# Attention and a two-layer network on one core: zero products and a small sigmoid at the start, two loads from another queue, and a wider choice of PSUM banks

## The chip, the cores and the metric

The kernel runs on one core of a Trainium2 chip. The metric is the device time of one execution in microseconds. A core has TensorE for matrix products, VectorE, ScalarE and GpSimd for elementwise work, and SyncE, from whose queue this kernel issues its transfers; each engine runs its own instructions in order and waits on semaphores for the others. TensorE writes only to PSUM, which the kernel uses as eight banks of 512 float32 columns.

## The reference

Eight batches, 12 heads, 448 positions, 64 columns a head. Attention takes a sigmoid in the place of a softmax; its output, laid out as 448 rows of 768, goes through a mixing of low rank along the sequence and then a two-layer network, both added on.

```python
scores = q @ k.T / sqrt(64) - log(448)
x = sigmoid(scores) @ v                    # heads side by side: (8, 448, 768)
u = x + ((x.T @ U) @ V).T                  # U (448, 32), V (32, 448)
out = u + relu(u @ w_ch1) @ w_ch2          # (768, 3072), (3072, 768)
```

## The kernel before

The 12 heads of a batch are worked off as six **pairs**. A pair's scores fill four tiles, j = 3, 0, 1, 2: three tiles of 128 keys for both heads, two banks each, and one bank that holds the last 64 keys of both heads. ScalarE's sigmoid brings each tile to SBUF, and TensorE multiplies with v. Batch 0 and half of batch 1 do this in float32; the rest, and all of the network, splits each float32 into two float16 parts and takes three products. The weights come as 64-bit words: VectorE decodes them in twelve groups (six for each layer, `decode`, L874), scales and splits them, and parks them in DRAM for the later batches. Batches 0 to 3 run the network in plain form (`ffn_in`, `ffn_out`), 4 to 7 in a form with seven products instead of eight, behind everything else.

The order is not written by hand. Every operation is handed to a `Plan` with an engine, an estimated cost, what it reads and writes, and a due position (`pos`). `Plan.order` (L136) plays the operations through in a model of the engines while the program is built: it always takes the operation that can start first, and among those that can start at the same time the one with the lowest due position. What it finds is then the fixed order of instructions on each engine and queue. So a changed due time, cost or choice of buffer changes the order on any engine. The due times come from constants at the head of the file (L54 to L77): `START` and `AT` place the network's groups, `D1` the pairs of batch 1, `TWO_AT` the attention of batch 2, `SOONER`, `B0` to `B5` that of batches 3 to 7, `PREP` and `BOUNDS` the preparation of a pair, `DECODE` the weights, `MIX_1`, `MIX_2` and `MIXED1` the mixing, `U_STEP` and `STEP_I` forms of inputs and weights for the last batches.

What the change and the prediction touch:

- `load` (L390) issues a transfer from SyncE's queue. `loads` (in front of `pair`, L537) brings a pair's k and q, each by head (64 partitions), into one of three `qk` buffers, and v into one of two.
- Batch 0's six pairs are the first work of TensorE, with due positions from -100 on. Between them run the decoding of the first weights, the mixing of batch 0 (`mix`) and, from 82 us, the first chains of the network.
- `mixing` (L496) sets up the identity, the sigmoid's bias and U and V; it writes `vst`, the scaled V in float16 (448 columns), late, at 67 us.
- PSUM: the network's chains take banks 0 to 3 (`PF`, L349) during the first pass over the groups; scores take banks 4 to 7, or all eight where `early` (L683) is true, that is in batch 0 and in pairs 0 and 1 of batch 1. A tile is given back once its last reader is done.
- Matmuls are issued on L407 and transposes on L410; VectorE's and ScalarE's helpers make L417, L420 and L679 stand for many operations.

Of the kernel before, what the change touches and what calls it, by code (L numbers as in the profile page):

```python
# [37 lines left out]
P = 128  # L38
D = 64
S = 448  # L40
# [10 lines left out]
DOWN = 2.0 ** -24  # L51
DOWN_H = 2.0 ** -22
WHOLE = (6, 6, 6, 0, 0, 0, 0, 0)
D2, TWO_AT = 24.207, 77.057  # L54
PLAIN = 4
LATER = [3, 4, 5, 6, 7]
TOGETHER = (2, 3, 4, 5)
# [4 lines left out]
PIPE = {P * PIECE * 8: 2.5, D * S * 4: 0.53, D * D * 4: 0.13, D * P * 4: 0.1, P * 2 * WE * 2: 4.8, P * 42 * P * 2: 4.1, P * 24 * P * 2: 1.92, P * 6: 2.2, P * 1536: 1.3}  # L62
SWITCH, TURN, LAND, RATE = 0.09, -2.054, 2.2, 0.33e6
TINY = 235
B0, B1, B2, B3, B4, B5 = 2.934, -0.318, -0.301, -2.832, -1.273, 1.274
HOLD_PE, HOLD_DVE, HOLD_ACT, HOLD_POOL, HOLD_SP = 0.029, 0.0, 0.0, 0.0, 0.0
HOLD = lambda e: {"PE": HOLD_PE, "DVE": HOLD_DVE, "ACT": HOLD_ACT, "POOL": HOLD_POOL, "SP": HOLD_SP}[e]

ROOM0, ROOM, AHEAD, BEFORE, D1, SOONER = 89.279, 30.792, 47.233, 54.769, 4.497, 70.468
PREP, BOUNDS, VALUES, SECOND, MIXED = 19.043, 11.533, 1.917, 3.17, 7.744  # L70
LOW_POOL = ()
MIXED1, MIX_1 = 1.829, -0.567
MIX_2, EV_IN, EV_OUT, A_OFF = 11.002, 33.543, 3.656, 0.056
START, DECODE = 30.42, 56.642
U_AT, U_STEP = 3.172, 3.581
LEAD, SUMS, STEP_K, STEP_I, FFN_LEAD = 5.196, 28.387, 3.783, 5.28, 4.0
ORDER = "iiiioiooiioiooiioiooiooo"  # L77


# [19 lines left out]
class Plan:  # L99
# [13 lines left out]
    def op(self, eng, cost, fn, reads=(), writes=(), pos=0.0, slack=0.0, land=0.12, after=(), port=False, dma=0.0, shape=(0, 0)):  # L113
        deps = set(after)
        for k in reads:
            deps.update(self.wrote.get(k, ()))
        for k in writes:
            deps.update(self.wrote.get(k, ()))
            deps.update(self.read.get(k, ()))
        i = len(self.ops)  # L120
        for k in reads:
            self.read.setdefault(k, []).append(i)
        for k in writes:
            self.wrote[k], self.read[k] = [i], []
        tiles = []
        for k in (*reads, *writes):
            t = k[0] if isinstance(k, tuple) else k
            if isinstance(t, Tile) and t not in tiles:
                tiles.append(t)
                t.users.append(i)  # L130
                if t.at is None:
                    t.at = (pos, i)
        self.ops.append((eng, cost, fn, sorted(deps), pos, slack, land, tiles, port, dma, shape))
        return i
# [123 lines left out]
def fused_kernel(ctx: ExitStack, tc: tile.TileContext, q, k, v, wu, wv, w1, w2, out):  # L258
# [128 lines left out]
            small[name] = [Buffer(tiny(n)) for _ in range(ring_)]  # L387
        return plan.tile(name, small[name])

    def load(dst, src, n, reads, writes, pos, land=LAND):  # L390
        op("SP", 0.6 if n in (D * S * 4, D * D * 4, D * P * 4) else 0.36, lambda: nc.sync.dma_start(out=dst(), in_=src()), reads, writes, pos, land=land, dma=PIPE.get(n, n / RATE))  # L391

    def dve(cost, fn, reads, writes, pos):
        op("DVE", cost, fn, reads, writes, pos)
# [5 lines left out]
    def act(cost, fn, reads, writes, pos):  # L400
        op("ACT", cost, fn, reads, writes, pos)
# [4 lines left out]
    def matmul(*x, **y):  # L406
        plan.made.append(nc.tensor.matmul(*x, **y))  # L407
# [109 lines left out]

    def shifted(at):  # L520
        pool(0.5, lambda: nc.gpsimd.memset(ux, 0.0), (), ["ux", "vraw"], at)
        dve(0.25, lambda: nc.vector.tensor_copy(ux[0:64, 0], ua[0:64, 3]), [("ua", i) for i in range(4)] + ["ux"], ["ux"], at)
        load(lambda: ux[64:128, :, 3], lambda: ua[0:64, :, 0], 0.08e6, [("ua", 0), "ux"], ["ux"], at)
        load(lambda: ux[0:64, 1:4, 3], lambda: ua[64:128, 0:3, 0], 0.08e6, [("ua", 0), "ux"], ["ux"], at)
# [12 lines left out]
    def loads(b, p, early, stacked):  # L537
        qk, v32 = plan.tile("qk", QK), plan.tile("v", V32)

        for h in range(2):  # L540
            for i, src in ((1, k), (0, q)):
                load(lambda i=i, h=h: qk.x[rows_of(h), i * S : i * S + S], lambda src=src, h=h: src[b, p, rows_of(h), h, :],
                     D * S * 4, [], [(qk, i, h)], early)
            if stacked:
                load(lambda h=h: qk.x[rows_of(h), 2 * S :], lambda h=h: kin[b, p, rows_of(h), h, S - D :], D * D * 4, [], [(qk, 2, h)], early)
        if stacked:
            x = v[b, p]
            ends = bass.AP(x.tensor, x.offset + 384, [[512, D], [512 * D + D, 2], [1, D]])
            load(lambda: v32.x[:, :3], lambda: v[b, p, :, :3], P * 384 * 4, [], [(v32, 0)], early + 0.1)
            for i in range(2):  # L550
                load(lambda i=i: v32.x[rows_of(i), 3, :], lambda: ends, D * P * 4, [], [(v32, 1 + i)], early + 0.1)
        else:
            load(lambda: v32.x, lambda: v[b, p], P * 512 * 4, [], [(v32, 0), (v32, 1), (v32, 2)], early + 0.1)
        return qk, v32, [(qk, i, h) for i in range(2) for h in range(2)]
# [48 lines left out]
    def pair(b, p, at, d):  # L603
# [76 lines left out]
                out_(), in_(), AF.Sigmoid, bias=bias_s, scale=c if whole else c.x), kin + ["bias"] + kc, kout, pos)  # L680

        sc = {}
        early = b == 0 or b == 1 and p < 2  # L683
        for n, j in enumerate((3, 0, 1, 2)):
            here = at + (d * (n // 2) / SECOND if b else 0.0)
            if b == 0:
# [35 lines left out]
    def new_u(b):  # L722
        u32s[b] = [plan.tile(f"u{'abc'[min(b, 2)]}{c}", [(UA, UB, UC)[min(b, 2)][c]]) for c in range(NP)]
        mxs[b] = sm("mx", NP) if b < PLAIN else sm(f"mx{b}", NP, 1)
# [511 lines left out]
            out_(u[0, 1], 1, 0)  # L1236


    mixing()
    new_u(0)  # L1240
    for p in range(NP):
        pair(0, p, 6.0 * p - 100.0, 6.0)
# [148 lines left out]
```

## Time and profile before

| | us |
|---|---|
| median of the timed runs | 1564.28 (1563.14 to 1565.6, three runs) |
| profiled execution | 1560.01 |
| its span | 1558.2 |
| TensorE busy in the span | 1548.8 |
| VectorE / ScalarE / GpSimd busy | 1112.4 / 776.1 / 351.5 |
| moved by DMA | 303.82 MB, 195 GB/s on average |

A profile is of one execution. A line of the order of time has the start in us from the span's start, the length, the engine, the line of the kernel, the operation, what it writes and reads (`out<-in`), its shape, how many like ones are merged into the line, and in brackets the idle time of the engine before it with what ended it. Names such as `qk__101` are buffers: the first pair's k and q. PE is TensorE's matmul part, PEld its loading of weights, DVE VectorE, ACT ScalarE, POOL GpSimd, SPq the queue of SyncE. A line of the view by stretches gives, for each stretch, its length and then the busy time of PE, PEld, DVE, ACT and POOL with their number of instructions, the granted clock, the share of the DMA engines' time and GB/s. A line of the waits gives the waiting engine, what it waited for, us in total, times, and the longest.

### The profile page before, as it was taken

To read this page: it belongs to the slowest core of one execution; us is meant where nothing else is said; L and a number is where in the kernel's file an instruction comes from. 1 tells how busy PE (TensorE), PEld (TensorE's weight loads), DVE (VectorE), ACT (ScalarE), POOL (GpSimd) and SP (SyncE) were. 2 spreads that over 40 slices of the span, in tenths; PEclk is the share of its full clock that TensorE was granted. 3 is DMA by queue.
4 is the path that set the end of the run, shared out by engine and by line. 5 is a ranking of instruction groups with operands and counts; after the bars stand their busy time and mean duration, and the time that the engine had idled before them with its cause. 6 is when DMAs were issued, how large, how long until landed. Compare 5 with 4: busy or idle time off the path is not lost.

```text
span 1558.2 us, 23417 instructions
## 1 busy us (share of the span) xinstructions
PE 1548.8 (99%) x8651; PEld 759.9 (49%) x8651; DVE 1112.4 (71%) x1831; ACT 776.1 (50%) x1269; POOL 351.5 (23%) x429
## 2 busy tenths in 40 slices
PE   8999999999999999999999999999999999999999
PEld 3334444455444454444444544555555555555554
DVE  4688987566667777787887677777767777565656
ACT  6566466444567557777878356342323614131310
POOL 0100000003551652221221451055662500000000
PEclk9999999999999999999999999999999999999999
DMA  9599777435658995776777775967773673333321
GB/s 280 174 310 316 220 265 242 148 96 159 184 153 220 250 280 145 204 174 168 183 222 221 213 244 161 264 217 238 237 253 137 212 259 108 107 109 140 107 106 72
DMA packets 217554, 303.82 MB, mean 195 GB/s; under 512 B 138336, under 2 KB 188384, under 8 KB 206176
## 3 DMA queue, kind: packets, MB, share of 16 engines
q1 hardware_dynamic: 217440, 302.33, 62.9%
q8 instruction: 68, 1.11, 0.3%
q14 instruction: 46, 0.38, 0.1%
HBM read 232.10 MB, written 76.04 MB: 198 GB/s over the span
## 4 chain that ended last, share of the span: by engine, by line
PE 57%; ACT 0%; DMA 0%; issue 0%; DVE 0%; SPq 0%; ACTq 0%
PE banks L407 57%; DMA v__105<-v_in 0%; ACT at L679 0%; PE banks L410 0%; ACT w L839 0%; ACT a L705 0%; DVE ub__79 L420 0%; SPq L391 0%; ACT junk L473 0%; ACTq L473 0%; DVE tiny L832 0%; ACT uc__83 L711 0%; DVE tiny L442 0%
## 5 line engine op out<-in xcount | busy, mean ns | idle before, releaser
L407 PEld LDWEIGHTS <-w__92 128*128 128x128 f16 x1683 | 163.3, 98 | 157.4 <-issue 6.7
L407 PEld LDWEIGHTS <-w__91 128*128 128x128 f16 x1620 | 157.0, 98 | 152.5 <-issue 8.5
L407 PEld LDWEIGHTS <-w__94 128*128 128x128 f16 x1620 | 157.0, 98 | 151.0 <-issue 8.6
L407 PEld LDWEIGHTS <-w__93 128*128 128x128 f16 x1557 | 150.4, 98 | 147.9 <-issue 11.5
L679 ACT ACTIVATE at<-banks,tiny 128x896 f32<-128x896 f32 x120 | 127.0, 1098 | 42.0 <-DVE a L420 18.9
L420 DVE SCALAR_TENSOR_TENSOR a<-at,a 64x896 f16<-64x896 f32 (+1 forms) x120 | 135.5, 1145 | 13.0 <-ACT a L705 8.3
L407 PE MATMUL banks<-h__96,w__94 128*128 128x448 f16 x690 | 139.7, 353 | 0.0
L407 PE MATMUL banks<-h__95,w__93 128*128 128x448 f16 x678 | 136.9, 353 | 0.4 <-ACT h__96 L939 0.4
L417 POOL TENSOR_SCALAR tiny<-tiny 128x1 f32<-128x1 f32 (+1 forms) x90 | 30.0, 342 | 354.4 <-DVE tiny L417 328.3
L1014 POOL TENSOR_TENSOR w<-w 128x384 f32<-128x384 f32 x96 | 105.8, 1102 | 5.2
L407 PE MATMUL banks<-us__89,w__92 128*128 128x448 f16 x498 | 101.3, 353 | 0.0
L407 PE MATMUL banks<-us__89,w__91 128*128 128x448 f16 x501 | 101.2, 353 | 0.0
L407 PE MATMUL banks<-us__90,w__91 128*128 128x448 f16 x471 | 95.1, 353 | 0.0
L407 PE MATMUL banks<-us__90,w__92 128*128 128x448 f16 x471 | 94.6, 353 | 0.0
L705 ACT ACTIVATE a<-at 128x896 f16<-128x896 f32 x90 | 82.6, 950 | 0.2
L679 ACT ACTIVATE a<-banks,tiny 128x448 f32<-128x448 f32 (+1 forms) x72 | 63.0, 910 | 27.6 <-PE banks L407 27.5
L1010 POOL TENSOR_TENSOR w<-w 128x384 f32<-128x384 f16 x48 | 46.6, 1000 | 95.5 <-DVE xnt L1018 70.7
L938 ACT ACTIVATE r__98<-banks 128x448 f32<-128x448 f32 x48 | 26.0, 541 | 70.6 <-PE banks L407 68.1
L938 ACT ACTIVATE r__97<-banks 128x448 f32<-128x448 f32 x48 | 25.9, 539 | 60.9 <-PE banks L407 60.7
L407 PE MATMUL banks<-h__95,w__94 128*128 128x448 f16 x264 | 54.3, 353 | 0.0
L407 PE MATMUL banks<-h__96,w__93 128*128 128x448 f16 x249 | 51.3, 353 | 0.0
L407 PEld LDWEIGHTS <-stg__109 64*128 64x128 f16 (+1 forms) x690 | 32.6, 102 | 38.1 <-issue 17.0
(897 smaller groups left out, 2833.0 us busy)
## 6 DMA issues: line engine op xcount, KB each, us to landing
w<-w_in SPq DMA_DIRECT2D x48, 768.0 KB, 6.2
forms<-xnt SPq DMA_DIRECT2D x24, 768.0 KB, 4.4
w__92<-forms SPq DMA_DIRECT2D x13, 1344.0 KB, 5.7
w__91<-forms SPq DMA_DIRECT2D x12, 1344.0 KB, 5.9
w__94<-forms SPq DMA_DIRECT2D x12, 1344.0 KB, 5.8
w__93<-forms SPq DMA_DIRECT2D x11, 1344.0 KB, 5.9
forms<-scratch SPq DMA_DIRECT2D x144, 96.0 KB, 5.0
w__91<-scratch SPq DMA_DIRECT2D x7, 1536.0 KB, 8.1
```

Of the source, the lines that this page charges most:

```text
L407: plan.made.append(nc.tensor.matmul(*x, **y))
L417: return eng.tensor_scalar(out=out, in0=in_, scalar1=s1, scalar2=s2, op0=op0, **kw)
L420: return nc.vector.scalar_tensor_tensor(out=out, in0=in0, scalar=s, in1=in1, op0=op0, op1=op1)
L679: act(cost, lambda: nc.scalar.activation(out_(), in_(), AF.Sigmoid, bias=bias_s, scale=c if whole else c.x), kin + ["bias"] + kc, kout, pos)
L705: act(0.95, lambda a=a, to=to: nc.scalar.activation(half(a, 0), to.x, AF.Copy, scale=A_UP), kto, [(a, 0)], here + A_OFF)
L938: act(0.54, lambda: nc.scalar.activation(r.x, ph.x[:, :S], AF.Relu, scale=DOWN_H), [ph], [r], pos - EV_IN)
L1010: pool(1.0, lambda j=j: nc.gpsimd.tensor_tensor(out=t.x[:, j], in0=quarter(j, 0), in1=quarter(j, 1), op=ALU.add), [(w, j, 0), (w, j, 1)] i ...
L1014: pool(1.0, lambda o_=o_, x=x, y=y, sub=sub: nc.gpsimd.tensor_tensor(out=t.x[:, o_], in0=t.x[:, x], in1=t.x[:, y], op=ALU.subtract if sub ...
```

## The change

Four things change.

1. Ahead of everything, VectorE sets `vst` to zero, and TensorE multiplies it with itself nine times into one bank (`waking`). The result isn't read; `vst` is written anew later.
2. ScalarE does a sigmoid of one column into `junk`, once the bias is there (`table`).
3. The two loads of q for pair 0 of batch 0 are issued from ScalarE's queue.
4. Pairs 2 and 3 of batch 1 count as `early`, so their scores may take all of PSUM. Beside it some fifteen of the constants for due times have other values.

```diff
@@ -51,7 +51,7 @@
 DOWN = 2.0 ** -24
 DOWN_H = 2.0 ** -22
 WHOLE = (6, 6, 6, 0, 0, 0, 0, 0)
-D2, TWO_AT = 24.207, 77.057
+D2, TWO_AT = 24.207, 73.828
 PLAIN = 4
 LATER = [3, 4, 5, 6, 7]
 TOGETHER = (2, 3, 4, 5)
@@ -62,18 +62,18 @@
 PIPE = {P * PIECE * 8: 2.5, D * S * 4: 0.53, D * D * 4: 0.13, D * P * 4: 0.1, P * 2 * WE * 2: 4.8, P * 42 * P * 2: 4.1, P * 24 * P * 2: 1.92, P * 6: 2.2, P * 1536: 1.3}
 SWITCH, TURN, LAND, RATE = 0.09, -2.054, 2.2, 0.33e6
 TINY = 235
-B0, B1, B2, B3, B4, B5 = 2.934, -0.318, -0.301, -2.832, -1.273, 1.274
+B0, B1, B2, B3, B4, B5 = 2.934, -0.318, -0.244, -3.203, -1.273, 1.299
 HOLD_PE, HOLD_DVE, HOLD_ACT, HOLD_POOL, HOLD_SP = 0.029, 0.0, 0.0, 0.0, 0.0
 HOLD = lambda e: {"PE": HOLD_PE, "DVE": HOLD_DVE, "ACT": HOLD_ACT, "POOL": HOLD_POOL, "SP": HOLD_SP}[e]
 
-ROOM0, ROOM, AHEAD, BEFORE, D1, SOONER = 89.279, 30.792, 47.233, 54.769, 4.497, 70.468
-PREP, BOUNDS, VALUES, SECOND, MIXED = 19.043, 11.533, 1.917, 3.17, 7.744
+ROOM0, ROOM, AHEAD, BEFORE, D1, SOONER = 89.279, 30.677, 47.233, 54.769, 4.497, 71.364
+PREP, BOUNDS, VALUES, SECOND, MIXED = 19.043, 11.364, 1.908, 3.17, 7.744
 LOW_POOL = ()
-MIXED1, MIX_1 = 1.829, -0.567
-MIX_2, EV_IN, EV_OUT, A_OFF = 11.002, 33.543, 3.656, 0.056
-START, DECODE = 30.42, 56.642
-U_AT, U_STEP = 3.172, 3.581
-LEAD, SUMS, STEP_K, STEP_I, FFN_LEAD = 5.196, 28.387, 3.783, 5.28, 4.0
+MIXED1, MIX_1 = 2.02, -0.414
+MIX_2, EV_IN, EV_OUT, A_OFF = 11.354, 33.543, 3.656, 0.056
+START, DECODE = 30.42, 55.967
+U_AT, U_STEP = 3.172, 3.587
+LEAD, SUMS, STEP_K, STEP_I, FFN_LEAD = 5.196, 28.387, 3.783, 5.157, 4.0
 ORDER = "iiiioiooiioiooiioiooiooo"
 
 
@@ -387,7 +387,10 @@
             small[name] = [Buffer(tiny(n)) for _ in range(ring_)]
         return plan.tile(name, small[name])
 
-    def load(dst, src, n, reads, writes, pos, land=LAND):
+    def load(dst, src, n, reads, writes, pos, land=LAND, other=False):
+        if other:
+            op("ACT", 0.6, lambda: nc.scalar.dma_start(out=dst(), in_=src()), reads, writes, -300.0, land=land + PIPE.get(n, n / RATE))
+            return
         op("SP", 0.6 if n in (D * S * 4, D * D * 4, D * P * 4) else 0.36, lambda: nc.sync.dma_start(out=dst(), in_=src()), reads, writes, pos, land=land, dma=PIPE.get(n, n / RATE))
 
     def dve(cost, fn, reads, writes, pos):
@@ -517,6 +520,19 @@
 
 
 
+    def waking():
+        bank = plan.tile("sc", BANK[:4], False)
+
+        def fn():
+            for _ in range(9):
+                matmul(bank.x[:, :S], vst[:, :P], vst, start=True, stop=True)
+
+        dve(0.15, lambda: nc.vector.memset(vst, 0.0), (), ["vst"], -300.0)
+        pe(3.2, fn, ["vst"], [bank], -300.0)
+
+    def table():
+        act(1.4, lambda: nc.scalar.activation(junk[:, :1], bias_s, AF.Sigmoid), ["bias"], ["warm"], -299.0)
+
     def shifted(at):
         pool(0.5, lambda: nc.gpsimd.memset(ux, 0.0), (), ["ux", "vraw"], at)
         dve(0.25, lambda: nc.vector.tensor_copy(ux[0:64, 0], ua[0:64, 3]), [("ua", i) for i in range(4)] + ["ux"], ["ux"], at)
@@ -540,7 +556,7 @@
         for h in range(2):
             for i, src in ((1, k), (0, q)):
                 load(lambda i=i, h=h: qk.x[rows_of(h), i * S : i * S + S], lambda src=src, h=h: src[b, p, rows_of(h), h, :],
-                     D * S * 4, [], [(qk, i, h)], early)
+                     D * S * 4, [], [(qk, i, h)], early, LAND, (b, p, i) == (0, 0, 0))
             if stacked:
                 load(lambda h=h: qk.x[rows_of(h), 2 * S :], lambda h=h: kin[b, p, rows_of(h), h, S - D :], D * D * 4, [], [(qk, 2, h)], early)
         if stacked:
@@ -680,7 +696,7 @@
                 out_(), in_(), AF.Sigmoid, bias=bias_s, scale=c if whole else c.x), kin + ["bias"] + kc, kout, pos)
 
         sc = {}
-        early = b == 0 or b == 1 and p < 2
+        early = b == 0 or b == 1 and p < 4
         for n, j in enumerate((3, 0, 1, 2)):
             here = at + (d * (n // 2) / SECOND if b else 0.0)
             if b == 0:
@@ -1236,7 +1252,9 @@
             out_(u[0, 1], 1, 0)
 
 
+    waking()
     mixing()
+    table()
     new_u(0)
     for p in range(NP):
         pair(0, p, 6.0 * p - 100.0, 6.0)
```

## The prediction

> **What bounds the kernel now.** I read the page's head first, then the waits of TensorE, then the busy time of a few stretches, then the first 18 us in order of time.
>
> ```profile
> span 1558.2 us, 23417 instructions
> PE 1548.8 (99%) x8651; PEld 759.9 (49%) x8651; DVE 1112.4 (71%) x1831; ACT 776.1 (50%) x1269; POOL 351.5 (23%) x429
> ...
> PE banks L407 <- DMA qk__101<-q_in: 4.3, 1, 4.3
> PE banks L407 <- ACT a L679: 1.0, 2, 0.6
> PE banks L407 <- ACT h__96 L939: 0.4, 1, 0.4
> PE banks L407 <- ACT at L679: 0.2, 1, 0.2
> ...
> 82.00:160.00 78.00, 77.64 (x392) 35.25 (x391) 65.10 (x115) 50.42 (x88) 0.00 (x0) 1.00 0.99 311
> 1009.00:1554.60 545.60, 545.58 (x2885) 281.96 (x2883) 367.95 (x580) 158.34 (x269) 118.81 (x114) 1.00 0.49 165
> ```
>
> TensorE is busy 1548.8 of 1558.2 us. All its waits are 5.9 us, and 4.3 of them are one wait at the very start, for the first q. What is left to take elsewhere is 1.0 + 0.4 + 0.2 = 1.6 us. Busy need not mean full speed, so I check the last stretch: 2885 matmuls in 545.58 us are 189 ns each, every one 128x128 and 448 columns wide, with no gap. So behind the first pairs the end is set by TensorE's own work in order, and a microsecond taken off the head of that line comes off the end, unless a later wait swallows it. The other stretch (82 to 160 us) is where that could happen: DMA share 0.99, VectorE busy 65 of 78 us.
>
> Then the start, TensorE's matmuls in order of time:
>
> ```profile
> 4.26 7.14 PE L407 MATMUL banks<-qk__101 64*64 64x448 f32 x16 [4.26 <-DMA qk__101<-q_in]
> 11.34 2.67 PE L407 MATMUL banks<-qk__102 64*64 64x448 f32 x12
> 13.94 3.42 PE L407 MATMUL banks<-a,v__104 128*128 128x448 f32 x14
> 17.29 1.02 PE L407 MATMUL banks<-qk__102 64*128 64x448 f32 x4
> 18.25 2.67 PE L407 MATMUL banks<-qk__103 64*64 64x448 f32 x12
> ```
>
> Each pair's scores are 16 of these instructions. The second pair's take 13.94 - 11.34 = 2.60 us for twelve and 18.25 - 17.29 = 0.96 for four: 3.56 us. The first pair's take 11.34 - 4.26 = 7.08. So 3.52 us of the start are neither waiting nor work that comes again. The weight loads say why:
>
> ```profile
> 4.23 0.28 PEld L407 LDWEIGHTS banks<-qk__101 64*64 64x64 f32 x2 [4.23 <-DMA qk__101<-k_in]
> 5.41 0.28 PEld L407 LDWEIGHTS banks<-qk__101 64*64 64x64 f32 x2 [0.90 <-DMA qk__101<-k_in]
> 7.09 0.50 PEld L407 LDWEIGHTS banks<-qk__101 64*128 64x128 f32 x4 [1.40 <-issue]
> ...
> 9.49 0.34 PEld L407 LDWEIGHTS banks<-qk__101 64*128 64x128 f32 x2 [0.41 <-issue]
> 10.24 0.34 PEld L407 LDWEIGHTS banks<-qk__101 64*128 64x128 f32 x2 [0.41 <-issue]
> 11.33 0.19 PEld L407 LDWEIGHTS banks<-qk__102 64*64 64x64 f32 x4 [0.75 <-issue]
> ...
> 12.72 0.19 PEld L407 LDWEIGHTS banks<-qk__102 64*128 64x128 f32 x2 [0.18 <-ACT a L679]
> 13.09 0.19 PEld L407 LDWEIGHTS banks<-qk__102 64*128 64x128 f32 x2 [0.18 <-issue]
> ```
>
> The same pair of loads comes every 10.24 - 9.49 = 0.75 us in the first pair and every 13.09 - 12.72 = 0.37 in the second. TensorE runs at half speed from 4.26 until about 10.9, though the granted clock of the stretch says 1.00 (the last but two of its columns):
>
> ```profile
> 0.00:11.34 11.34, 7.08 (x17) 2.43 (x17) 0.00 (x0) 3.66 (x4) 1.18 (x8) 1.00 0.66 210
> ```
> A second loss is in the first two rows of the loads: the second head starts at 5.41, over a microsecond behind the first, as its k and q are issued third and fourth.
>
> The Trainium skill, "TensorE: Matmul & The Clock Gate" (Part 1), says that the array starts at half rate and is released at the end of a busy window of about 3.4 us that runs freely and doesn't start with the kernel. The trace agrees on the factor (0.75 against 0.37 us); that the moment of release drifts from run to run one profile can't show.
>
> **The change part by part.** Sums are made against the profiled execution, 1560.01 us, which is its span and 1.8 us around it. The three timed runs have a median of 1564.28, which is 4.3 above it, and differ by 2.5 among themselves; I move the median by the same difference.
>
> *Loads.* The two first q go from SyncE's queue to ScalarE's.
>
> ```profile
> 0.72 0.60 SPq L391 DMA_DIRECT2D qk__101<-k_in  x1
> 1.38 0.58 SPq L391 DMA_DIRECT2D qk__101<-q_in  x1
> 1.99 0.60 SPq L391 DMA_DIRECT2D qk__101<-k_in  x1
> 2.63 0.60 SPq L391 DMA_DIRECT2D qk__101<-q_in  x1
> ```
>
> Issued at 1.38, the first q lets the matmul go at 4.26: 2.88 us. Issued beside the k at 0.72, it is there at about 3.6, and the second head's pair (issued at 1.38 on each queue, 2.8 later as 5.41 - 2.63) at 4.2. Everything behind them on SyncE moves up by the two issues, 1.25 us, v and the first weights too; ScalarE has nothing else then, and the two issues cost it 1.3 us. ScalarE's own stall in the start:
>
> ```profile
> 7.25 1.28 ACT L679 ACT_TABLE_LOAD   x1 [7.25 <-PE banks L407]
> 8.54 1.53 ACT L679 ACTIVATE a<-banks,tiny 128x448 f32<-128x448 f32 x2
> ```
>
> The load of the table moves into idle time, to about 2.0 to 3.3 us. Before, it cost nothing: the first values begin at 13.94 with no wait. With a first pair that is 3 us faster TensorE comes to the values at 10.9; table and four sigmoids (1.3 + 4 x 0.85, the mean of the two quoted and the 0.91 of the group quoted below) from about 5.9, where the first scores are done, would end at 10.6. So I count the one-column sigmoid at zero; without it the gain would be used up to the last 0.3 us. The Trainium skill, "ScalarE: Activation LUTs" (What ACT_TABLE_LOAD costs), gives 1.28 us for the load and 1.38 more for a drain. The trace has the first part, and the next instruction starts at 8.54, right where the load ends, so no drain is seen; by that page 1.4 us more would be protected.
>
> *Products of zeros.* VectorE clears vst, TensorE does nine 128x128 products of 448 columns.
>
> ```profile
> 1.26 0.52 POOL L509 MEMSET ub<- 128x512 f16 x1
> 67.07 0.44 DVE L417 TENSOR_SCALAR vst<-vraw,tiny 128x448 f16<-128x448 f32 x1
> ```
>
> VectorE's clearing isn't in the trace. A like one on GpSimd takes 0.52 us, a 448-column write on VectorE 0.44, so it lies between 0.1 (the 1-column ones) and 0.5: TensorE begins at 0.9 to 1.3, I take 1.2. Nine products at half speed are 9 x 2 x 0.189 = 3.4 us, so they end at 4.6, 0.4 behind the data. They replace idle time and delay the scores by that 0.4.
>
> When does full speed come? Two counts from the rows. (a) As long after the first work as before, 10.9 - 4.26 = 6.6 us: at 1.2 + 6.6 = 7.8. (b) As long after the first work that fills the array's 128 columns, 10.9 - 7.09 = 3.8 us: at 5.0. In (a) half-speed work from 4.6 to 7.8 does 1.6 of the 3.56 us, the rest ends at 9.8: 1.6 us gained on 11.34. In (b) 0.2 are done by 5.0 and the pair ends at 8.3: 3.0 gained. I take (b), as the products fill the array like the work from 7.09 on. The clock rule of the skill gives release between 1.2 + 3.4 and 1.2 + 6.8 by chance, and an estimate of 3.2 to 1.5 us gained; it would put the likeliest gain nearer 2.4.
>
> *Does the next thing follow?* The second pair's loads (last issued at 5.69 before, 4.4 now, some 3.6 to land) are there by 8.1, about when the first pair ends. The third pair's, and the buffers given back, move with TensorE. I count nothing.
>
> *PSUM and the constants.* Pairs 2 and 3 of batch 1 may put scores into all eight banks, and some fifteen due times and steps change by up to a few microseconds, which reorders all queues behind the start. The matmuls stay the same ones. Since TensorE waits only 1.6 us behind its first matmul, the best that any order can bring is 1.6 us; the worst has no such bound and is a rival. I take zero.
>
> Sum: -3.0 us, 1560.0 to 1557.0 in a profiled execution, 1564.28 - 3.0 = **1561.3** in the timed runs.
>
> **The rivals.** *Order helps too.* The start's 3.0 and the 1.6 of waits left: 1564.28 - 4.6 = 1559.7. For it: more banks and a later start of batch 2 are the sort of thing that takes out waits for ScalarE's sigmoid (1.0 of the 1.6). Against: a new order can make new waits as easily.
>
> *The products don't wake the array* (zeros don't count as work). Then the scores start at 4.6 with both heads at half speed, the first score tile takes 1.5 us, and full speed comes 3.8 us after it, at 9.9; by then (9.9 - 4.6) / 2 = 2.65 are done and the rest ends at 10.8: 0.5 gained, 1563.8. Only a few tenths come from the loads, as the products end after them.
>
> *Given back at the weights.* VectorE finishes the second group's weights just ahead of their use:
>
> ```profile
> 99.81 0.56 DVE L417 TENSOR_SCALAR stg__109<-w 128x768 int32<-128x768 int32 x1 [3.57 <-DMA w<-w_in]
> ...
> 108.91 1.01 DVE L420 SCALAR_TENSOR_TENSOR w__92<-stg__109,tiny,w__92 128x768 f16<-128x768 f32 x1
> ...
> 110.28 2.07 PE L407 MATMUL banks<-us__89,w__92 128*128 128x448 f16 x10
> ```
>
> They are ready at 109.92, used at 110.28. If this end doesn't move, as loads fill the DMA (0.99), TensorE waits 2.6 of the 3.0 us: 1563.9. Against it: SyncE's loads move up 1.25 us from the start, and TensorE can be given attention work first.
>
> *Slower: scores hold the FFN's banks.* Before, pairs 2 to 5 of batch 1 leave banks 0 to 3 to the FFN. Now six two-bank score tiles of pairs 2 and 3 may sit there until their sigmoid is done.
>
> ```profile
> L679 ACT ACTIVATE a<-banks,tiny 128x448 f32<-128x448 f32 (+1 forms) x72 | 63.0, 910 | 27.6 <-PE banks L407 27.5
> L938 ACT ACTIVATE r__98<-banks 128x448 f32<-128x448 f32 x48 | 26.0, 541 | 70.6 <-PE banks L407 68.1
> ```
>
> If an FFN chain meets such a tile, it waits for the sigmoid and the two evictions queued ahead of it on ScalarE, 0.91 + 2 x 0.54 = 2.0 us; six times that is 12, less 3.0: 1573. It ends slower from about 1.0 us a tile on (6.1 in all: the 3.0 and the 3.1 of a measurable loss). Against: a score group before never waited in that part, so four banks were enough, and the FFN's chains follow one another with no gap.
>
> **How the numbers follow.** 0.2% of 1564.28 is 3.1 us, about what a measurement can tell from no change; the line to faster lies at 1561.15, beside my forecast. Chances: forecast 0.40 (count (b), or a bit on either side: half of it 0.18 faster, 0.22 same), order helps too 0.27, zeros don't wake 0.13, given back 0.10, banks held 0.10. So faster 0.45, same 0.45, slower 0.10. The range goes from 1557.8 (order helps, and the 1.2 us that the runs differ either way, with some rest) to 1565.0 (no gain, and the same). It leaves out the banks and the far ends of the others, under 0.2.
>
> **What would show it.** Right: nine matmuls from vst before 4.6 us, weight loads of the first pair at 0.37 us from the second tile of scores on, the second pair starting at 8.1 to 9.8 instead of 11.34, the table load before 4 us, waits of TensorE behind the start at 1.6 us or less, and the last matmul 3 us earlier. Wrong: loads still at 0.75 us after 8 us (zeros don't count); a wait at the first use of w__92 or for banks between 180 and 260 us; more waits on ScalarE than before; or a time under 1558, which neither the start nor the waits could pay for.

## The result and the profile after

The change makes the kernel slower. The median goes from 1564.94 us (four runs beside it) to 1585.6 us (1584.14 to 1587.48), a ratio of 1.0129 with a 95% interval of 1.0107 to 1.0152: some 20.7 us. The forecast was 1561.3, its range 1557.8 to 1565.0. Neither the direction nor the size was in it.

The head of the page after (line numbers have moved: L407 is L410 now, L679 is L695, L417 is L420, L420 is L423):

```profile
span 1582.3 us, 23465 instructions
PE 1557.1 (98%) x8660; PEld 761.3 (48%) x8660; DVE 1155.4 (73%) x1832; ACT 774.9 (49%) x1270; POOL 396.0 (25%) x429
```

Against before TensorE has nine matmuls more, the products of zeros, VectorE and ScalarE one instruction more each. GpSimd has none more. And yet VectorE is busy 43 us longer (1112.4 before) and GpSimd 44.5 us longer (351.5 before), ScalarE 1.2 us shorter. Keep these two numbers in mind: they are the fingerprint that the experiments follow.

The waits of TensorE after, as the prediction read them for before:

```profile
PE banks L410 <- DMA w<-w: 4.7, 3, 3.6
PE banks L410 <- ACT a L695: 2.6, 2, 2.0
PE banks L410 <- ACT h__96 L955: 1.8, 1, 1.8
PE banks L410 <- ACT ua__74 L727: 1.7, 1, 1.7
PE banks L410 <- DVE ub__80 L423: 1.6, 1, 1.6
PE banks L410 <- DVE stg__109 L423: 1.2, 1, 1.2
```

Before, all waits behind the first matmul came to 1.6 us, and none was for VectorE. Now there are many, of up to 3.6 us, on the transposing transfers, ScalarE and VectorE (the first lines of the list are shown). No wait is long enough to be "the" cause. The view by stretches says where they lie (length, then busy time of PE, PEld, DVE, ACT, POOL, the granted clock, DMA share, GB/s). Before:

```profile
0.00:20.00 20.00, 15.74 (x54) 5.37 (x56) 5.99 (x8) 10.15 (x14) 1.18 (x8) 1.00 0.82 251
20.00:160.00 140.00, 138.69 (x651) 56.68 (x648) 107.96 (x199) 90.20 (x151) 10.22 (x10) 1.00 0.87 273
160.00:1010.00 850.00, 849.77 (x5073) 416.39 (x5071) 630.51 (x1048) 517.47 (x839) 221.27 (x297) 1.00 0.68 200
1010.00:1540.00 530.00, 530.00 (x2803) 274.09 (x2802) 359.41 (x567) 158.23 (x268) 118.81 (x114) 1.00 0.49 167
```

After:

```profile
0.00:20.00 20.00, 18.13 (x69) 6.05 (x69) 5.51 (x8) 10.97 (x16) 1.18 (x8) 1.00 0.91 250
20.00:160.00 140.00, 134.68 (x625) 55.21 (x625) 108.60 (x199) 84.25 (x142) 10.07 (x10) 0.99 0.89 273
160.00:1010.00 850.00, 838.33 (x4981) 407.66 (x4979) 639.36 (x1024) 514.57 (x836) 259.47 (x297) 1.00 0.69 196
1010.00:1540.00 530.00, 527.26 (x2787) 272.55 (x2786) 375.97 (x562) 160.95 (x272) 125.23 (x114) 1.00 0.51 173
```

Length less busy time of PE is what TensorE idles: from 20 to 160 us 5.3 after against 1.3 before, from 160 to 1010 us 11.7 against 0.2, from 1010 to 1540 us 2.7 against 0. So 18.1 us of idle time came in, most of it hundreds of microseconds behind the start and behind batch 1's banks. GpSimd's 259.47 against 221.27 shows that the extra busy time lies in the same stretch.

Some waits cost twice. In three stretches after, the granted clock (last but two) is 0.96, where before has 1.00 in the same stretches:

```profile
80.00:120.00 40.00, 38.65 (x173) 14.77 (x175) 34.98 (x55) 26.88 (x46) 2.81 (x3) 0.96 1.03 313
440.00:480.00 40.00, 38.29 (x242) 17.84 (x242) 32.40 (x44) 29.16 (x45) 21.42 (x19) 0.96 0.86 192
520.00:560.00 40.00, 39.20 (x210) 19.24 (x209) 26.87 (x49) 15.85 (x33) 18.00 (x21) 0.96 0.84 215
```

Behind a wait the array runs at half speed for a while, by the trace's records of when the granted clock changed (its clock records) for 3.41 us each time (82.94 to 86.35, 475.47 to 478.88, 519.84 to 523.26). In order of time, fourteen instructions on values after,

```profile
81.35 5.11 PE L410 MATMUL banks<-a,v__105 128*128 128x448 f32 x14 [1.96 <-ACT a L695]
```

take 5.11 us; the same group takes 3.42 at full speed (quoted from before in the prediction, at 13.94). That is 1.7 us lost on top of a wait of 1.96 (half of 3.41), and three such places make 5.1.

Now the start, the part that the prediction worked out. TensorE's matmuls after, in order of time, and then some of its loads of weights:

```profile
1.14 3.48 PE L410 MATMUL banks<-vst 128*128 128x448 f16 x9 [1.14 <-DVE vst L530]
4.55 0.96 PE L410 MATMUL banks<-qk__101 64*64 64x448 f32 x2
6.25 3.39 PE L410 MATMUL banks<-qk__101 64*64 64x448 f32 x14 [0.74 <-DMA qk__101<-k_in]
9.57 2.67 PE L410 MATMUL banks<-qk__102 64*64 64x448 f32 x12
```

```profile
4.54 0.19 PEld L410 LDWEIGHTS banks<-qk__101 64*64 64x64 f32 x2 [0.67 <-issue]
...
7.59 0.19 PEld L410 LDWEIGHTS banks<-qk__101 64*128 64x128 f32 x2 [0.18 <-issue]
7.97 0.19 PEld L410 LDWEIGHTS banks<-qk__101 64*128 64x128 f32 x2 [0.18 <-issue]
```

The products run from 1.14 to 4.6. The first load of real weights takes 0.19 us and not 0.28, so the array is at full speed by 4.54; the pairs of loads come every 0.38 us from then on. The second pair starts at 9.57 against 11.34: the start gains 1.77 us, and the table's load, too, lies at 1.96 to 3.25 us as intended.

So the last matmul, 24.1 us later than before (1578.7, as no idle time is left behind 1540 us, against 1554.6), comes about like this: 1.8 off at the start, 4.0 + 11.4 + 2.7 on in the three stretches behind it, and 5.1 for the half speed make 21.4. The other 2.7 I can't put down to rows.

### The profile page after: what moved, and what is told of

Same layout as the page of the kernel before. It is cut to its first block, busy times and chain, and to the rows that moved or that the text cites. A ratio compares the mean times of both kernels' runs of the same rounds, so it can differ in the third digit from the quotient of the medians.

```text
span 1582.3 us, 23465 instructions
## 1 busy us (share of the span) xinstructions
PE 1557.1 (98%) x8660; PEld 761.3 (48%) x8660; DVE 1155.4 (73%) x1832; ACT 774.9 (49%) x1270; POOL 396.0 (25%) x429
## 4 chain that ended last, share of the span: by engine, by line
PE 81%; DMA 7%; DVE 7%; SPq 2%; issue 2%; ACT 1%; POOL 1%; DVEq 0%; ACTq 0%; POOLq 0%
PE banks L410 80%; DMA row__114<-far 2%; DMA w<-w_in 2%; SPq L394 1%; DVE a L423 1%; DMA forms<-xnt 1%; SPq L857 1%; DMA w__91<-scratch 1%; DMA v__104<-v_in 1%; DMA far<-tiny 1%; DVE w L423 1%; PE banks L413 0%; DVE xnt L1034 0%; DVE tiny L480 0%; ACT at L695 0%
## 5 line engine op out<-in xcount | busy, mean ns | idle before, releaser
L410 PEld LDWEIGHTS <-w__92 128*128 128x128 f16 x1683 | 163.2, 98 | 161.5 <-issue 11.5
L410 PEld LDWEIGHTS <-w__91 128*128 128x128 f16 x1620 | 157.5, 98 | 153.6 <-issue 8.9
L410 PEld LDWEIGHTS <-w__94 128*128 128x128 f16 x1620 | 156.3, 98 | 155.7 <-issue 15.9
L410 PEld LDWEIGHTS <-w__93 128*128 128x128 f16 x1557 | 150.9, 98 | 148.1 <-issue 12.4
L423 DVE SCALAR_TENSOR_TENSOR a<-at,a 64x896 f16<-64x896 f32 (+1 forms) x120 | 141.7, 1194 | 15.1 <-ACT a L718 8.4
L695 ACT ACTIVATE at<-banks,tiny 128x896 f32<-128x896 f32 x120 | 126.9, 1098 | 30.3 <-PE banks L410 16.4
L410 PE MATMUL banks<-h__95,w__93 128*128 128x448 f16 x687 | 140.4, 354 | 1.1 <-DVE ua__72 L423 1.1
L420 POOL TENSOR_SCALAR tiny<-tiny 128x1 f32<-128x1 f32 (+1 forms) x90 | 46.9, 531 | 373.9 <-DVE tiny L420 347.2
L410 PE MATMUL banks<-h__96,w__94 128*128 128x448 f16 x678 | 138.9, 356 | 0.1
L1030 POOL TENSOR_TENSOR w<-w 128x384 f32<-128x384 f32 x96 | 110.4, 1150 | 4.6
L410 PE MATMUL banks<-us__90,w__91 128*128 128x448 f16 x507 | 104.0, 353 | 0.0
L410 PE MATMUL banks<-us__90,w__92 128*128 128x448 f16 x507 | 103.7, 353 | 0.0
L410 PE MATMUL banks<-us__89,w__92 128*128 128x448 f16 x495 | 100.9, 353 | 1.8 <-ACT h__96 L955 1.8
L410 PE MATMUL banks<-us__89,w__91 128*128 128x448 f16 x498 | 101.6, 353 | 0.0
L1026 POOL TENSOR_TENSOR w<-w 128x384 f32<-128x384 f16 x48 | 50.1, 1074 | 112.0 <-DVE xnt L1034 86.2
L695 ACT ACTIVATE a<-banks,tiny 128x448 f32<-128x448 f32 (+1 forms) x72 | 62.8, 910 | 29.8 <-PE banks L410 29.6
L410 PE MATMUL banks<-h__95,w__94 128*128 128x448 f16 x264 | 54.9, 353 | 0.0
L410 PEld LDWEIGHTS <-stg__109 64*128 64x128 f16 (+1 forms) x690 | 32.6, 101 | 39.7 <-issue 17.1
L410 PEld LDWEIGHTS <-stg__108 64*128 64x128 f16 (+1 forms) x690 | 32.6, 101 | 39.6 <-issue 18.3
```

What stands on the lines that cost most here:

```text
L420: return eng.tensor_scalar(out=out, in0=in_, scalar1=s1, scalar2=s2, op0=op0, **kw)
L423: return nc.vector.scalar_tensor_tensor(out=out, in0=in0, scalar=s, in1=in1, op0=op0, op1=op1)
L695: act(cost, lambda: nc.scalar.activation(out_(), in_(), AF.Sigmoid, bias=bias_s, scale=c if whole else c.x), kin + ["bias"] + kc, kout, pos)
L1026: pool(1.0, lambda j=j: nc.gpsimd.tensor_tensor(out=t.x[:, j], in0=quarter(j, 0), in1=quarter(j, 1), op=ALU.add), [(w, j, 0), (w, j, 1)] i ...
L1030: pool(1.0, lambda o_=o_, x=x, y=y, sub=sub: nc.gpsimd.tensor_tensor(out=t.x[:, o_], in0=t.x[:, x], in1=t.x[:, y], op=ALU.subtract if sub ...
```

## The experiments

The theory after this reading: the start does what it should, and the loss comes with another order of everything behind it. The rivals: the nine products and the moved loads harm something later; the wider choice of banks holds the network up; the new constants are a worse plan. Times are medians, each with its ratio to runs of the kernel before on the same chip; the ratio weighs all runs and is not exactly the quotient of the two medians.

**The start, in the order of before.** The order of all other instructions is kept. The products are added by hand ahead of it, the sigmoid right behind the setting of the bias, and the two loads stay at their places but go to ScalarE's queue.

```diff
-        op("SP", ..., lambda: nc.sync.dma_start(out=dst(), in_=src()), ...)
+        op("SP", ..., lambda: (nc.scalar if other else nc.sync).dma_start(out=dst(), in_=src()), ...)
...
+            nc.scalar.activation(junk[:, :1], bias_s, AF.Sigmoid)
...
     with tc.manual_schedule():
+        nc.vector.memset(vst, 0.0)
+        for _ in range(9):
+            nc.tensor.matmul(BANK[7].ap[:, :S], vst[:, :P], vst, start=True, stop=True)
         plan.emit(tc)
```

> Kernel before with the zero products, the one-column sigmoid and the two q loads from ScalarE's queue put in front of an otherwise unchanged order of every engine; constants and banks as before. Theory A (the loss comes from the new order, the start is good): 1.5 to 2 us under the kernel before, as in the changed kernel the second pair starts at 9.57 in the place of 11.34; TensorE's waits behind the start stay under 2.5 us. Theory B (the earlier start itself drives TensorE into weights and transfers that do not move): all of it given back or more, equal to the kernel before up to 20 us slower.

Measured: 1566.13 us against 1564.99, ratio 1.0005 (0.9991 to 1.002). The start's instructions harm nothing and bring nothing that shows. The second pair starts at 9.97 us here, 1.4 earlier than before, but TensorE then stops where it did not stop before:

```profile
37.79 1.02 PE L407 MATMUL banks<-qk__102 64*128 64x448 f32 x4
40.63 1.02 PE L407 MATMUL banks<-qk__102 64*128 64x448 f32 x4 [1.82 <-ACT ua__74 L715]
41.59 1.92 PE L407 MATMUL banks<-qk__103 64*64 64x448 f32 x8
44.27 1.92 PE L407 MATMUL banks<-a,v__104 128*128 128x448 f32 x6 [0.76 <-ACT a L683]
```

What ScalarE does just ahead of that, in order of time:

```profile
39.21 0.84 ACT L473 ACTIVATE junk<-us__90 128x768 bf16<-128x768 f32 x1 [2.43 <-DVE us__90 L420]
...
40.05 0.53 ACT L715 ACTIVATE ua__74<-banks 128x448 f32<-128x448 f32 x1
40.48 1.00 ACT L683 ACTIVATE a<-banks,tiny 128x896 f32<-128x896 f32 x1
```

and VectorE:

```profile
36.57 0.56 DVE L417 TENSOR_SCALAR us__90<-w 128x768 int32<-128x768 int32 x1 [2.02 <-DMA w<-w_in]
37.16 1.95 DVE L420 SCALAR_TENSOR_TENSOR us__90<-w,us__90 128x768 int32<-128x768 int32 x2
```

ScalarE works in order. The bound of a piece of weights stands first in its queue and waits 2.43 us for VectorE's decoding, which itself had waited 2.02 us for the transfer; the eviction and the sigmoid that TensorE needs stand behind it. Before, VectorE begins the same decoding at 35.46 (2.15 us of wait), 1.1 us earlier: issuing the weights earlier did not bring them earlier in this execution. The first piece was issued at 6.29 against 6.96 and landed at 12.82 against 12.18; the two pieces that are waited for here landed at 36.55 and 39.72 against 35.43 and 38.18.

**The start, planned anew.** Points 1 to 3 of the change, with the constants and the banks of before.

```diff
+    waking()
     mixing()
+    table()
```

> The same start, but handed to the planner, which orders everything anew; constants and banks as before. Theory A with the constants as the cause: 1 to 2 us under the kernel before. Theory A with any new order as the cause: several us over it, 5 to 20. Theory B: slower as well, by as much as with the kept order.

Measured: 1581.68 us, ratio 1.0096 (1.0072 to 1.0119). Nearly all the loss, without constants or banks. VectorE is busy 1160.5 us, GpSimd 399.3. Between this kernel and the one above lies only what the planner decides: the order, and with it which buffer a tile gets. Below, "the order" means both.

**The constants alone, the banks alone.** Two kernels, each before with one part of the change: the values at the head of the file, or this line.

```diff
-        early = b == 0 or b == 1 and p < 2
+        early = b == 0 or b == 1 and p < 4
```

> Kernel before with the new constants for due times alone, start and banks as before. Constants as the cause: 15 to 25 us over the kernel before, with waits of TensorE for transposing transfers and sigmoids from 360 us on. Banks or start as the cause: within 3 us of it.

> Kernel before with all of PSUM for pairs 2 and 3 of batch 1 alone. Banks as the cause: 10 us or more over the kernel before, with waits of TensorE from 180 to 260 us. Constants as the cause: within 3 us. Any new order as the cause: some us over it, with waits at places that have nothing to do with batch 1's scores.

Measured: 1563.71 (0.9989, 0.9977 to 1.0001) and 1563.31 (0.9993, 0.9981 to 1.0004). Neither can be told from before. VectorE is at 1112.9 and 1115.8 us, GpSimd at 350.3 and 349.7.

**The order alone.** The plan of the second kernel, with nothing in the place of the start's operations: the planner sees an operation on VectorE, TensorE and ScalarE, but no instruction comes of it, and q is loaded from SyncE's queue.

```diff
+        dve(0.15, lambda: None, (), ["vst"], -300.0)
+        pe(3.2, lambda: None, ["vst"], [bank], -300.0)
...
+        act(1.4, lambda: None, ["bias"], ["warm"], -299.0)
```

> The order that the planner finds for the new start (TensorE's order as in the second run but for the zero products), with none of the start's instructions: no zero products, no early sigmoid, q from SyncE's queue; constants and banks as before. Theory A' (the order alone costs the time): 12 to 20 us over the kernel before, the same waits behind 80 us as in the second run (0.6 to 2.2 us each at the evictions and at 1040 to 1210 us). Theory B' (order and earlier start cost it together): under 8 us over.

Measured: 1582.18 us against 1564.23, ratio 1.0114 (1.0095 to 1.0133); VectorE 1160.0 us, GpSimd 398.6. The loss is there without one of the start's instructions. It is the order.

**The change without its constants, without its banks.** Each is the change with that part put back.

> The changed kernel with the old constants: start and banks. If the new order by the start is the whole cause and the rest adds little: 1578 to 1586, as the second run and the changed kernel. If the constants make it worse once the start is in: some 4 us under the changed kernel; if banks help or harm the order, outside of that on either side.

> The changed kernel with batch 1's banks as before: start and constants. If the start's order is the cause: 1578 to 1590. If the new constants were a remedy for the start's order: 1570 or less. If the loss needs the banks: near the kernel before.

Measured: 1573.95 (1.0064, 1.0048 to 1.0079) and 1587.01 (1.0142, 1.0128 to 1.0157). In the new order the constants do matter: the change's are 11.7 us worse than those of before (1585.6 less 1573.95; the two intervals, 1.0107 to 1.0152 and 1.0048 to 1.0079, lie apart), though alone they did nothing. With the change's constants the banks still do nothing that shows. Without these constants they may help: the start with the banks (1573.95) is 7.7 us under the start without them (1581.68, planned anew, above), though the two intervals just touch (1.0048 to 1.0079, 1.0072 to 1.0119). Without the banks the constants cost 5.3 us (1587.01 less 1581.68). So what they cost depends on the rest of the order.

**The start's gain, followed one step.** The first kernel with the two bounds moved behind the eviction and the sigmoid that they held up, on ScalarE's queue alone.

```diff
+        for j, n in ((6, 2), (7, 1)):
+            i = self.bounds[j]
+            at = order.index(i)
+            to = [m for m in range(at + 1, len(order)) if self.ops[order[m]][0] == "ACT"][n - 1]
+            order.insert(to, order.pop(at))
```

> The first run's kernel (order kept, new start) with ScalarE's two bounds of the second weights' last two pieces moved behind the next eviction and sigmoids, so that these no longer stand behind a weight that has not come. Theory (the start's gain is held up at 40 us by a weight's arrival in ScalarE's queue): the waits of 1.8 and 0.8 us at 40 and 44 us go, and the time is 1.5 to 2.5 us under the first run, 1 to 2 under the kernel before. Rival (the gain would be lost further on anyway, at 82, 111 or 142 us, where weights arrive): equal to the first run within 0.7 us, with the waits moved.

Measured: 1564.53 us against 1564.23, ratio 1.0006 (0.9992 to 1.0019). The two waits near 40 us are gone (one of 0.22 us at 42.20 is left), and the next one stands a little later:

```profile
53.35 3.42 PE L413 MATMUL banks<-a,v__105 128*128 128x448 f32 x14 [1.24 <-ACT a L689]
```

There is another of 1.85 us at 143.05. But this run can't tell where a gain would go. In its profiled execution the second pair starts at 11.15 us, so there was only 0.2 us to lose, and the two pieces of weights landed at 34.41 and 37.52, 2.1 and 2.2 us earlier than in the run above, so the waits may have gone for that reason too. What would have to move for the end to move was not found.

**Who goes first at equal times.** Why does a start of three operations reorder a kernel of thousands? In `Plan.order` the candidates lie in a dictionary by engine:

```python
        free, cand = {}, {}
        for i, o in enumerate(self.ops):
            free.setdefault(o[0], 0.0)
            cand.setdefault(o[0], [])
        ...
            for e, c in cand.items():
                ...
                    if best is None or t < best[0]:
                        best = t, e, now
```

Within an engine the lowest due position goes first. Between engines, at equal times, the one goes first that was put in first, as `<` doesn't replace it. That is the engine of the first operation ever handed over. Before, `mixing` came first and its first operation is GpSimd's: GpSimd, SyncE, VectorE, TensorE, ScalarE. `waking` begins with VectorE's clearing of `vst`, so now VectorE leads. It matters since the planner lets instructions of VectorE and GpSimd that share a port (`port`) wait for each other: when both wait for it, their times are equal. Playing `Plan.order` through for the kernel before gives 210 steps at which VectorE and GpSimd share the first place, 188 of them because both wait for the port. In the planner's model the orders cost nearly the same: it ends TensorE's work at 1562.4 us for before, at 1562.8 with VectorE first and at 1561.0 for the change.

Two kernels test it from both sides. The first is before, with VectorE put in first and nothing else changed:

```diff
-        free, cand = {}, {}
+        free, cand = {"DVE": 0.0}, {"DVE": []}
```

> The kernel before, whose planner is told to look at VectorE ahead of GpSimd when both could start at the same moment; no other line changes, no instruction is added. Theory C (putting an operation of VectorE first in the plan turned the order of the engines in the planner's ties, and that alone is the loss): 12 to 20 us over the kernel before, VectorE busy 1150 to 1165 us and GpSimd 393 to 405, as in the changed kernel, in the place of 1112 and 352. Rival D (the loss comes from the start's times or buffers in the plan): within 3 us of the kernel before, VectorE and GpSimd as before.

Measured: 1579.05 us against 1565.01, ratio 1.0079 (1.0066 to 1.0093). No instruction has come or gone. The head of its page:

```profile
span 1576.7 us, 23399 instructions
PE 1553.0 (98%) x8651; PEld 760.1 (48%) x8651; DVE 1160.1 (74%) x1831; ACT 774.6 (49%) x1269; POOL 397.3 (25%) x429
```

The second is the whole change, with the engines put in as they came before:

```diff
-        free, cand = {}, {}
+        free, cand = {e: 0.0 for e in ("POOL", "SP", "DVE", "PE", "ACT")}, {e: [] for e in ("POOL", "SP", "DVE", "PE", "ACT")}
```

> The changed kernel with all its parts, but with the planner's ties looked at in the order of the kernel before (GpSimd, SyncE, VectorE, TensorE, ScalarE). Theory C: the loss goes, 1560 to 1567, VectorE busy 1110 to 1120, GpSimd 348 to 356, TensorE's waits behind the start under 8 us. Rival D: 1575 to 1587, as the changed kernel.

Measured: 1566.25 us against 1565.01, ratio 1.0005 (0.9992 to 1.0017).

```profile
span 1565.0 us, 23439 instructions
PE 1550.6 (99%) x8660; PEld 760.7 (49%) x8660; DVE 1113.0 (71%) x1832; ACT 774.9 (50%) x1270; POOL 352.2 (23%) x429
```

The loss appears with the tie rule alone and goes with it alone. A place where it shows plainly on GpSimd are three scalings of 128x448 near 80 us. In order of time, before:

```profile
77.37 1.35 POOL L417 TENSOR_SCALAR us__89<-ua__72,tiny 128x448 f16<-128x448 f32 x1 [8.50 <-DVE tiny L442]
78.69 2.35 POOL L417 TENSOR_SCALAR us__89<-ua__74,tiny 128x448 f16<-128x448 f32 x1
81.02 0.64 POOL L417 TENSOR_SCALAR us__89<-ua__76,tiny 128x448 f16<-128x448 f32 x1
```

Before, with VectorE first at equal times:

```profile
80.52 1.84 POOL L417 TENSOR_SCALAR us__89<-ua__72,tiny 128x448 f16<-128x448 f32 x1 [8.50 <-DVE tiny L442]
82.34 1.00 POOL L417 TENSOR_SCALAR us__89<-ua__74,tiny 128x448 f16<-128x448 f32 x1
83.32 1.00 POOL L417 TENSOR_SCALAR us__89<-ua__76,tiny 128x448 f16<-128x448 f32 x1
```

The same three instructions take 1.35, 2.35 and 0.64 us in one order and 1.84, 1.00 and 1.00 in the other. The start with the order kept and the change with the old ties have 1.35, 2.35, 0.64 again, the change itself 2.17, 1.00, 1.00.

**Constants and banks without the start.** The change with `waking`, `table` and the loads taken out, so that GpSimd comes first again.

> Constants and banks of the changed kernel without the start. With theory C: 1560 to 1565, as each of the two alone (0.9989 and 0.9993 of the kernel before), and so the rest of the change is worth 0 to 3 us. If the start's 1.5 to 2 us were kept with these constants, this run would be 1.5 to 2 us over the one before it in this list; if the weights' transfers hold it up at 40 us all the same, equal to it within 1 us.

Measured: 1565.74 us, ratio 1.0002 (0.999 to 1.0014). VectorE 1112.7 us, GpSimd 349.0.

All of it side by side, with the idle time of TensorE from 160 to 1540 us worked out from the view by stretches as above:

| kernel | first at equal times | us | VectorE / GpSimd busy | idle 160 to 1540 |
|---|---|---|---|---|
| before | GpSimd | 1564.94 | 1112.4 / 351.5 | 0.2 |
| start, order kept | GpSimd | 1566.13 | 1113.1 / 354.0 | 0.6 |
| the same, two bounds moved | GpSimd | 1564.53 | 1110.5 / 353.3 | 1.6 |
| constants alone | GpSimd | 1563.71 | 1112.9 / 350.3 | 0 |
| banks alone | GpSimd | 1563.31 | 1115.8 / 349.7 | 0 |
| no start | GpSimd | 1565.74 | 1112.7 / 349.0 | 0 |
| change, old ties | GpSimd | 1566.25 | 1113.0 / 352.2 | 2.0 |
| change | VectorE | 1585.6 | 1155.4 / 396.0 | 14.4 |
| before, VectorE first | VectorE | 1579.05 | 1160.1 / 397.3 | 7.9 |
| start, planned anew | VectorE | 1581.68 | 1160.5 / 399.3 | 8.7 |
| order alone | VectorE | 1582.18 | 1160.0 / 398.6 | 8.6 |
| change without constants | VectorE | 1573.95 | 1162.4 / 402.2 | 8.6 |
| change without banks | VectorE | 1587.01 | 1156.7 / 396.5 | 12.8 |

The two groups don't touch in any column. None of the kernels beats before by more than a measurement can tell.

## Why the prediction was wrong

*What bounds the kernel.* Right, and the reason why the loss is so plain: TensorE was busy from end to end, so new waits went to the end. What the start gained in the order of before did not: a later wait swallowed it, as the prediction allowed.

*The loads.* Half right. The first head's k and q landed at 3.90 (forecast 3.6), and the products held its scores until 4.55. The second head was to be there at 4.2. Its q landed at 5.87 and its k at 6.11, though issued 1.3 and 0.6 us earlier than before, where they landed at 5.31 and 4.67. Its matmuls waited until 6.25, and in the start with the order kept until 6.66; before, its loads of weights started at 5.41. So issuing earlier, on two queues, did not bring the second head earlier, and the wait for it (0.74 us) is more than half of the 1.27 us by which the second pair missed the forecast. That "the first weights too" would move up was wrong in the same way: issued at 6.11 instead of 6.96, the first piece landed at 13.10 instead of 12.18.

*The products of zeros.* Right on what they do, wrong on the sum. They run from 1.14 to 4.6 (forecast 1.2 to 4.6), and zeros do release the clock: that rival (0.13) is out. Full speed came at 4.43 by the trace's clock record, earlier even than the 5.0 of count (b). That was in part luck: in the six other kernels with the products it came at 3.91 to 6.18, in those without them at 9.96 to 12.31; that it came for count (b)'s reason, the filled array, no run shows. The wait for the second head then made the second pair start at 9.57, where I had 8.3. So 1.77 us were gained instead of 3.0; that this is near the 1.6 of count (a) is chance. In the six other kernels with the start the second pair began at 8.87 to 11.15 us: a gain of 2.5 at best, 0.2 at worst.

*The table.* Right: off the path before and after.

*"Does the next thing follow?"* Wrong. "I count nothing" overlooked ScalarE's queue near 40 us, where the decoding of the weights holds up what TensorE needs. The rival "given back at the weights" had the mechanism, on the decoding and its transfers, but put it at 110 us; it came at 40 us, ahead of the first use of `w__92`. With the order kept the whole gain of the start is given back, and 1563.9 of that rival is within 2.4 us of the 1566.13 and 1566.25 measured.

*PSUM and the constants.* **This is the step that failed**: "the best that any order can bring is 1.6 us; the worst has no such bound and is a rival. I take zero." Zero was right for the constants and banks themselves (1563.71 and 1563.31 alone, 1565.74 together), so the rival "order helps too" (0.27) didn't come either, and the banks' rival (0.10, waits from 180 to 260 us) was not what happened: the change without its banks is as slow as with them. But the term for a new order was put at nothing with only due times in view that move "by up to a few microseconds". The start itself reorders the kernel, by being the first to be handed to the planner, and I took it for an addition ahead of an order that stays. My description of the planner carries the error: among the operations that can start at the same time the lowest due position wins, it says. That holds within an engine; between engines the dictionary decides. The prediction had seen that the worst "has no such bound", and priced only the banks of it. The order's own share is 14.0 us with the constants of before (1579.05 less 1565.01; 12.4 by the ratio) and 19.4 with those of the change (1585.6 less 1566.25).

*What would show it.* The list named "more waits on ScalarE than before", and those came; it named none on VectorE or the transposing transfers, and none behind 260 us, where most of the loss is.

What is shown is that the tie rule makes the loss. How the other order makes it, is less sharp. GpSimd's largest groups, before (busy us, mean ns of one, idle before):

```profile
L1014 POOL TENSOR_TENSOR w<-w 128x384 f32<-128x384 f32 x96 | 105.8, 1102 | 5.2
...
L417 POOL TENSOR_SCALAR tiny<-tiny 128x1 f32<-128x1 f32 (+1 forms) x90 | 30.0, 342 | 354.4 <-DVE tiny L417 328.3 <-DVE tiny L868 16.8 <-ACT h__95 L939 3.8
```

and with VectorE first:

```profile
L1014 POOL TENSOR_TENSOR w<-w 128x384 f32<-128x384 f32 x96 | 115.2, 1200 | 5.0
...
L417 POOL TENSOR_SCALAR tiny<-tiny 128x1 f32<-128x1 f32 (+1 forms) x90 | 39.3, 447 | 332.0 <-DVE tiny L417 329.4 <-ACT uc__83 L711 0.3
```

The same 96 and the same 90 instructions are 9.4 and 9.3 us longer in sum. Taken instruction by instruction, the two traces say when. An instruction that runs while the other of the two engines is idle takes the same in both orders: a sum of 128x384 (L1014) on GpSimd 1.00 us, a combination of 128x896 (L420) on VectorE 1.09. One that runs while the other engine is busy takes longer, 1.13 and 1.31 on average before, 1.21 and 1.25 with VectorE first. And there are more of them: GpSimd works at the same time as VectorE for 224 us before and for 320 with VectorE first (221 to 227 in all seven kernels with GpSimd first, 313 to 327 in the six with VectorE first). By how much the overlapping instructions exceed the median of their kind alone (the shortest of the kind where none ran alone) comes to 34.9 us on VectorE and 54.4 on GpSimd before, and to 78.3 and 99.9 with VectorE first. These 43.4 and 45.5 us more are nearly the whole extra busy time (47.7 and 45.8). Not all instructions are affected: VectorE's reductions of 128x448 take 0.61 us either way.

So in the other order the two engines run into each other more often, and the extra busy time lies where they do; the planner's model, with its fixed costs, has no such price. That longer chains over both are the source of TensorE's new waits is still argued: no run took the contention away and kept the order, and the change without its constants has the most overlap of all (327 us) with the smallest loss of its group. Why the change's constants cost 11.7 us in the new order and nothing in the old one is open, too. In the profiles, 5.8 us of it are idle time behind 160 us (14.4 against 8.6) and 5.1 the three stretches at half speed, of which the kernel without the constants has none.

## What to carry to other kernels

Where a planner writes the order, an edit is never local: before pricing a few instructions at the head, find out by which rule ties are broken, and whether the edit changes that rule's input. When a result is far from the sum of the parts, run the order without the instructions and the instructions without the order; here two runs settled it. And busy times of engines that the change doesn't touch, with the same number of instructions, are the quickest sign that the order has moved.

## What the runs showed of the hardware

*Half speed comes back after short waits, but not after each.* In the change without its constants the same group as at 81.35 above waits as long and runs at full speed:

```profile
82.03 3.42 PE L410 MATMUL banks<-a,v__105 128*128 128x448 f32 x14 [1.96 <-ACT a L695]
```

Both had a wait of 1.96 us; one lost 1.7 us more, one nothing. In the clock records of all kernels, each stretch at half speed between the start and the last matmul lasts 3.41 us, or twice that (6.83, once, in the order alone). The Trainium skill, "TensorE: Matmul & The Clock Gate" (Part 1), has the clock watched in windows of 3413 ns that run freely, and half rate return after an idle window of about that length. The dependence on the moment agrees; a wait of 1.96 us is well below such a window, and was enough here.

*The same products release the clock, but it doesn't always hold.* With the bounds moved, the products ran from 1.14 as ever, and yet the first pair's fourteen instructions took 5.08 us instead of 3.39:

```profile
4.29 0.96 PE L413 MATMUL banks<-qk__101 64*64 64x448 f32 x2
6.13 5.08 PE L413 MATMUL banks<-qk__101 64*64 64x448 f32 x14 [0.88 <-DMA qk__101<-q_in]
11.15 2.67 PE L413 MATMUL banks<-qk__102 64*64 64x448 f32 x12
```

The first two instructions, 0.96 us, are at full speed as in the change (0.96). The clock records have full speed from 3.91 to 7.32, half speed from 7.32 to 10.74 and full speed from there on: it fell back one stretch of 3.41 us after the release, in which lay a wait of 0.88 us and the first head's two instructions alone. The second pair starts at 11.15, and only 0.2 us is left of the gain. In the change, with a wait of 0.74 us at nearly the same place, it held. So in these two runs a warm-up ahead of a wait was a matter of luck with the moment.

*VectorE and GpSimd pay for each other.* The same instructions of each engine cost 40 to 53 us more in the one order than in the other (1155.4 to 1162.4 against 1110.5 to 1115.8, and 396.0 to 402.2 against 349.0 to 354.0 in the table above). The Trainium skill, "SBUF — State Buffer" (SBUF: two separate sides), describes a pair of ports that both share and that one holds for a whole instruction while the other is blocked. The traces agree in that the extra time lies in instructions that overlap with the other engine's (224 us of overlap against 320, as told above), and the triple of 1.35, 2.35 and 0.64 against 1.84, 1.00 and 1.00 us is what such waiting might look like; no run here isolates the port.
